# First batches loaded ahead of the weights, the start written out step by step, and the up weights' lower parts moved from GpSimd to VectorE

## The chip, the core and the metric

The kernel runs on one core of one Trainium2 chip. A core has a matrix engine (TensorE, "PE" in the rows, with its weight loads shown apart as "PEld"), a vector engine (VectorE, "DVE"), a scalar engine (ScalarE, "ACT"), GpSimd ("POOL") and a queue engine (SyncE, "SP") that here only issues DMAs. The engines run their own instruction streams in order and wait for one another through semaphores. The metric is the device time in microseconds, the median of three runs.

## The reference

```python
def _attn_ref(q, k, v):                       # (4, 8, 768, 64) each
    ...
    for t in range(S):
        state = gamma * state + einsum('bhd,bhe->bhde', k[:, :, t], v[:, :, t])
        y[:, :, t] = scale * einsum('bhd,bhde->bhe', q[:, :, t], state)

def _moe_ref(x, w_a, w_b, w_out):             # x 3072x512, d_ff 1536
    return (x @ w_a) * (x @ w_b) @ w_out

def _moe2_ref(x, w_gate, w_output_gate, w1, w2):   # 8 experts, 512 -> 1024 -> 512
    e_idx = argmax(x @ w_gate)
    ...
    out[mask] = gate_w * eom * (relu(x[mask] @ w1[e]) @ w2[e])
```

A decaying linear attention over 768 steps, a gated feed-forward layer, and a mixture of eight experts with one expert per token, chained on 3072 tokens, all in float32.

## The kernel before

**Blocks.** The tokens go through in seven blocks, block 0 to 6, most of 512 tokens. A block's feed-forward part loops over 12 slices `f` of the hidden width: `proj(j, f, 0, n)` and `proj(j, f, 1, n)` are two projections of 12 matmuls each, `gate` multiplies them, and `down` adds the slice into four accumulators with another 12 matmuls. Between them, in slots, stands the attention of the next block. So block 0 needs its own attention first, with nothing to overlap, and this stretch is called the start here.

**Three matmuls for one.** Every float32 operand is split into a high part (a cast by ACT) and a lower part (operand minus high part). `mm3` (L104 to L107) issues high by high, high by lower, lower by high. The first two need the high part of the weights, the third (L107) the lower part.

**The attention of a batch.** A batch is two heads pairs of 256 tokens. `load_batch(n)` brings two 512 KB tiles, `qk` and `vk`; `prep_q` and `prep_v` scale them (L139, L146) on DVE or POOL by the sets in L47; `scores` is 64 small matmuls in two tiles, masked by DVE (L189), with four running states added by DVE (L192) and a carry by POOL (L195); `outputs` is 64 small matmuls, two copies by ACT (L217) and two adds by DVE (L220). For block 0 the result `z` is then split into `xs` (L223 ACT, L224 DVE). Block 0 needs batches 0 to 3; the slots of block 0 do batches 4 to 7.

**Narrowing.** The weights of the feed-forward layer arrive as pairs of 32-bit words, 512 KB for each of 36 tiles. `narrow_all` (L473) makes floats of them: two reads by ACT (`narrow_a`, `narrow_r`), two joins by DVE (L487 and L489), then the high part by ACT (L457) and the lower part by POOL (L458). Twelve of the 36 are the down weights (`wos`), which are also written back to DRAM for later blocks; 24 are the up weights in `arena`. `narrow_all` is a generator, and `narrow(k)` advances it by k steps, from the third step of the start and three times per slice of block 0. A tile's slot in `wide` (4 deep) comes free with its second join, which is when `next_wide` issues the next load.

**Order.** All instructions are issued in the order in which the code is written (`tc.manual_schedule()`); the pools decide only the waits for buffers. Runs of small dummy matmuls (`keep_warm`, L783) stand between the steps of the start. SP issues the DMAs in order: batches 0 and 1, a weight tile, batch 2, three weight tiles, batches 3 and 4 (L786 to L799, L244).

Of the kernel before, what the change touches and what calls it, by code (L numbers as in the profile page):

```python
# [7 lines left out]
F32 = mybir.dt.float32  # L8
# [36 lines left out]
NARROW_FROM, CONST_AT = 2, 5  # L45

Q_POOL, V_POOL = {1, 2, 3}, {2, 3}  # L47
# [6 lines left out]
def attention_moe_moe2(ctx: ExitStack, tc: tile.TileContext, a: dict, out: bass.AP):  # L54
# [8 lines left out]
    e3 = early.enter_context(tc.tile_pool(name="e3", bufs=2))  # L63
    e5 = early.enter_context(tc.tile_pool(name="e5", bufs=3))
# [3 lines left out]
    def lp(n):  # L68
        if not late:
            for _ in narrowing:  # L70
                pass
# [64 lines left out]
    def prep_q(n):  # L136
        c, pp = batches[n]
        qd = p2.tile([128, 2, 256], F32, tag="qd", name="qd")
# [3 lines left out]
    def prep_v(n):  # L142
        c, pp = batches[n]
        vd = p2.tile([128, 2, 4, 64], F32, tag="vd", name="vd")
# [4 lines left out]
    spare = ["p0", "p1", "acc0", "acc1", "acc2"]  # L149

    def attn_bank(name):
        if not spare:
# [44 lines left out]
    def outputs(n, xr, toff):  # L197
# [20 lines left out]
        for i in range(2):  # L218
            zi = z[:, :, cols].rearrange("p k (j i n) -> p k j i n", j=2, i=2)[:, :, :, i]
            dve.tensor_tensor(zi, zi, y[i][:, 256:].rearrange("p (k j n) -> p k j n", k=2, j=2), op=ALU.add)  # L220
        if xr is None:
            hi, lo = (xs[:, w, 2 * pp : 2 * pp + 2, toff : toff + 256] for w in range(2))
            act.copy(hi, z)  # L223
            dve.tensor_tensor(lo, z, f32(hi), op=ALU.subtract)  # L224
# [7 lines left out]
    def attention_steps(j):  # L232
        own = [(ci, 2 * c + pp) for ci, c in enumerate(BLOCKS[j]) for pp in range(2)]

        def put(ci, n):
            if j == 0:
                xraw[j] = None
            elif j not in xraw:
# [3 lines left out]
        def s_a(n):  # L242
            scores(n)
            m = {0: 3, 1: 4, 2: None}.get(n, n + 2)  # L244
            if m and m < len(batches):
                load_batch(m)
# [7 lines left out]
        if j == 0:  # L254

            for i, (ci, n) in enumerate(own):
                steps.append(lambda n=n: s_a(n))
                if i:
                    steps.append(lambda p=own[i - 1], nxt=n + 1: s_b(*p, nxt if nxt <= len(own) else None))
            steps.append(lambda: s_b(*own[-1], None))  # L260
        else:
            for i, (ci, n) in enumerate(own):

                nxt = n + 1 if n + 1 < len(batches) and not (j == 1 and i + 1 == len(own)) else None
                steps.append(lambda n=n: s_a(n))
# [739 lines left out]
```

## Time and profile before

| | us |
|---|---|
| median of three runs | 1033.81 (1032.15 to 1034.11) |
| profiled execution | 1037.62 |
| its span, first to last instruction | 1035.7 |
| PE busy in the span | 1003.5 |
| start of the first projection matmul of block 0 | 37.14 |
| start of the second projection of slice 0 | 43.28 |
| start of the first projection of slice 1 | 46.15 |
| start of the first projection of block 1 | 155.74 |

The span is one profiled execution, 3.8 us slower than the median; some 1.9 us of the execution's time lie outside the span. A row of the timeline gives start, duration, engine, line, operation, tiles, and in brackets how long the engine had been idle before it and which instruction ended that. A group row gives busy time, mean duration in nanoseconds, and the idle time before. Matmuls are pipelined: one of 512 columns is shown as 0.39 us long, but the next starts some 0.23 us after it.

### The profile page before, as it was taken

What the parts mean: (1) busy time and instruction counts of PE and PEld (TensorE: products, weight loads), DVE (VectorE), ACT (ScalarE), POOL (GpSimd) and SP (SyncE); (2) the same over time, 40 slices, a digit from 0 to 9 for tenths busy, and PEclk for the clock granted to TensorE, in tenths of its full rate; (3) what the DMA queues carried; (4) which work ended last, traced back from release to release, by engine and by line L of the source; (5) the groups of instructions that cost most, each with busy time, mean ns of one, the idle gap of its engine ahead of it and who ended that gap; (6) DMA issues with size and microseconds to landing.
All of it is one profiled execution on the core that took longest, in us unless ns stands there. A gap on an engine that the chain in (4) does not pass through costs nothing. (4 is left out here: it accounts for less than half of the span.)

```text
span 1035.7 us, 20318 instructions
## 1 busy us (share of the span) xinstructions
PE 1003.5 (97%) x7701; PEld 840.1 (81%) x7702; DVE 606.6 (59%) x1383; ACT 382.3 (37%) x775; POOL 276.8 (27%) x241
## 2 busy tenths in 40 slices
PE   6799999999999999999999999999999999999997
PEld 4687778887888788888888888999899888789886
DVE  5799886755577547664775584453355444345441
ACT  3466662222322242223222323453354434344431
POOL 1455541113211421123113334341321120221211
PEclk7799999999999999999999999999999999999999
DMA  8676745322432342234221432360564552545620
GB/s 328 204 235 209 227 131 169 135 81 55 154 112 81 94 163 93 82 98 138 83 92 52 127 99 72 119 188 31 155 209 144 176 173 84 182 129 162 187 87 28
DMA packets 51640, 138.99 MB, mean 134 GB/s; under 512 B 10909, under 2 KB 11165, under 8 KB 51488
## 3 DMA queue, kind: packets, MB, share of 16 engines
q1 hardware_dynamic: 43920, 117.16, 35.3%
q0 software_dynamic: 6864, 19.46, 6.0%
q8 instruction: 85, 1.39, 0.5%
q10 hardware_dynamic: 720, 0.57, 0.2%
q14 instruction: 51, 0.42, 0.1%
HBM read 121.37 MB, written 16.70 MB: 133 GB/s over the span
## 5 line engine op out<-in xcount | busy, mean ns | idle before, releaser
L105 PE MATMUL p<-xs,arena 128*128 128x512 f32 (+1 forms) x672 | 248.5, 370 | 8.1 <-DVE z L220 4.2
L107 PE MATMUL p<-xs,arena 128*128 128x512 f32 (+1 forms) x672 | 242.5, 361 | 0.6 <-POOL arena L458 0.6
L106 PE MATMUL p<-xs,arena 128*128 128x512 f32 (+1 forms) x672 | 242.5, 361 | 0.0
L515 POOL TENSOR_TENSOR wos<-wo,wos 128x512 fp32r<-128x512 f32 x72 | 99.5, 1383 | 282.7 <-ACT wos L514 280.1
L105 PEld LDWEIGHTS p<-xs,arena 128*128 128x128 f32 x672 | 127.2, 189 | 31.8 <-issue 9.6
L107 PEld LDWEIGHTS p<-xs,arena 128*128 128x128 f32 x672 | 127.3, 190 | 20.7 <-POOL arena L458 1.0
L106 PEld LDWEIGHTS p<-xs,arena 128*128 128x128 f32 x672 | 127.5, 190 | 18.7
L542 ACT CAST gs<-g_sb 128x512 fp32r<-128x512 f32 (+1 forms) x84 | 47.0, 559 | 211.8 <-DVE g_sb L540 209.5
L340 DVE SCALAR_TENSOR_TENSOR junkd<-x,wcol 128x512 bf16<-128x512 f32 x144 | 122.0, 847 | 3.6
L105 PE MATMUL acc<-wos,gs 128*128 128x512 f32 x288 | 115.5, 401 | 0.0
L107 PE MATMUL acc<-wos,gs 128*128 128x512 f32 x288 | 113.3, 393 | 0.0
L106 PE MATMUL acc<-wos,gs 128*128 128x512 f32 x288 | 112.8, 392 | 0.0
L671 DVE TENSOR_TENSOR arena<-wraw,arena 128x512 fp32r<-128x512 f32 x112 | 76.2, 689 | 56.5 <-ACT arena L670 48.7
L637 DVE SCALAR_TENSOR_TENSOR hs<-ph,hs 128x384 fp32r<-128x384 f32 (+4 forms) x72 | 39.0, 542 | 113.6 <-ACT hs L636 87.7
L540 DVE TENSOR_TENSOR g_sb<-p,a_sb 128x512 f32<-128x512 f32 (+1 forms) x84 | 51.3, 611 | 79.4 <-PE p L107 70.2
L657 POOL DMA_INDIRECT out<-y,idx x27 | 27.5, 1018 | 234.9 <-ACT y L656 193.4
L105 PE MATMUL acc<-arena,hs 128*128 128x512 f32 (+1 forms) x216 | 86.1, 399 | 3.6 <-issue 1.9
L670 ACT CAST arena<-wraw 128x512 fp32r<-128x512 f32 x112 | 68.0, 616 | 57.7 <-PE acc L107 42.2
L107 PE MATMUL acc<-arena,hs 128*128 128x512 f32 (+1 forms) x216 | 85.8, 397 | 0.0
L106 PE MATMUL acc<-arena,hs 128*128 128x512 f32 (+1 forms) x216 | 85.3, 395 | 0.0
L543 DVE TENSOR_TENSOR gs<-g_sb,gs 128x512 fp32r<-128x512 f32 (+1 forms) x84 | 52.1, 620 | 52.5 <-ACT gs L542 51.2
L636 ACT ACTIVATE hs<-ph 128x384 fp32r<-128x384 f32 (+4 forms) x72 | 34.5, 479 | 127.0 <-PE ph L107 106.9
(147 smaller groups left out, 1687.0 us busy)
## 6 DMA issues: line engine op xcount, KB each, us to landing
wraw<-in_ex SPq DMA_DIRECT2D x64, 512.0 KB, 3.7
wo<-wo_d SPq DMA_DIRECT2D x72, 256.0 KB, 2.6
wide<-in_w_ab SPq DMA_DIRECT2D x24, 512.0 KB, 4.3
qk<-in_qk SPq DMA_DIRECT2D x23, 512.0 KB, 4.2
vk<-in_vk SPq DMA_DIRECT2D x23, 512.0 KB, 6.8
wcol<-in_wgt SPq DMA_DIRECT2D x20, 512.0 KB, 4.5
wide<-in_w_out SPq DMA_DIRECT2D x12, 512.0 KB
x_d<-x SPq DMA_DIRECT2D x24, 256.0 KB, 2.1
```

The costliest lines, as they stand in the source:

```text
L105: pe.matmul(outp, lhsT=wh, rhs=rh, start=start, stop=False)
L106: pe.matmul(outp, lhsT=wh, rhs=rl, start=False, stop=False)
L107: pe.matmul(outp, lhsT=wl, rhs=rh, start=False, stop=stop)
L340: dve.scalar_tensor_tensor(junk, x2t[i], 1.0, wc[:, e], op0=ALU.mult, op1=ALU.mult, accum_out=st["lg"][:, e0 + e : e0 + e + 1])
L515: pool.tensor_tensor(w[:, 1], t, f32(w[:, 0]), op=ALU.subtract)
L540: dve.tensor_tensor(g[:, :n], pb[:, :n], ta[:, :n], op=ALU.mult)
L542: act.copy(gs[:, 0, :n], g[:, :n])
L543: dve.tensor_tensor(gs[:, 1, :n], g[:, :n], f32(gs[:, 0, :n]), op=ALU.subtract)
L636: act.activation(h[:, 0, :n], p[:, :n], AF.Relu)
L637: dve.scalar_tensor_tensor(h[:, 1, :n], p[:, :n], 0.0, f32(h[:, 0, :n]), op0=ALU.max, op1=ALU.subtract)
L670: act.copy(arena[:, f, part, 0], t[:, part])
L671: dve.tensor_tensor(arena[:, f, part, 1], t[:, part], f32(arena[:, f, part, 0]), op=ALU.subtract)
```

## The change

The start is written out step by step in place of the loop over `attention_steps(0)`. Batches 0, 1 and 2 are loaded before the first weight tile, batch 3 before the second. Batches 2 and 3 have buffers of their own for their scaled operands (a `wos` buffer is borrowed), and both operands are scaled by POOL (`V_POOL` takes in 1). The first four batches use seven PSUM banks in turn, not five. `scores(n + 1)` stands in front of `outputs(n)`. `outputs` for block 0 hands back its three steps (join, high, lower), and the lower parts of batches 0 to 2 go to POOL, that of batch 3 to DVE. Narrowing has four functions of a tile's number: `n_read` (ACT), `n_join` (DVE, the first join now in place over the tile that ACT wrote), `n_high` (ACT), `n_low`. The lower part of an up weight is computed by DVE, that of a down weight by POOL. The reads run four tiles ahead, the joins three. The order of the 36 tiles has the down weight of a slice behind the up weights of the next one. The constants are loaded in slice 1 of block 0, not in the start.

```diff
-NARROW_FROM, CONST_AT = 2, 5
-
-Q_POOL, V_POOL = {1, 2, 3}, {2, 3}
+Q_POOL, V_POOL = {1, 2, 3}, {1, 2, 3}
...
-    e3 = early.enter_context(tc.tile_pool(name="e3", bufs=2))
-    e5 = early.enter_context(tc.tile_pool(name="e5", bufs=3))
+    e3 = early.enter_context(tc.tile_pool(name="e3", bufs=3))
+    e5 = early.enter_context(tc.tile_pool(name="e5", bufs=5))
...
+        if n in (2, 3):
+            both = p2.tile([128, 2, 512], F32, tag="wos", name="prep")
...
-    spare = ["p0", "p1", "acc0", "acc1", "acc2"]
+    spare = ["p0", "p1", "acc0", "acc1", "acc2", "gen", "gen"]
...
-    wide = [("ab", 0, 0), ("ab", 0, 1), ("wide", 0), ("ab", 1, 0), ("ab", 1, 1)]
+    wide = [("ab", 0, 0), ("ab", 0, 1)]
     for f in range(NF1):
-        wide += [("ab", f + 2, 0), ("ab", f + 2, 1)] if f + 2 < NF1 else [None, None]
-        wide += [("wide", f + 1)] if f + 1 < NF1 else []
-    wide = [k for k in wide if k]
+        wide += [("ab", f + 1, 0), ("ab", f + 1, 1)] if f + 1 < NF1 else []
+        wide += [("wide", f)]
...
+    def n_read(n):
+        if n < len(wide):
+            t = rawq[wide[n]]
+            e = e5.tile([128, 512], F32, tag="w_cv", name="w_cv")
+            act.activation(e, t[:, :, 1].bitcast(F32), AF.Copy, scale=REBIAS)
+            r = e3.tile([128, 512], I32, tag="r_cv", name="r_cv")
+            act.activation(r, t[:, :, 0].bitcast(U32), AF.Copy, scale=0.875 * 2.0**-29, bias=0.4999)
+            words[n] = e, r
+
+    def n_join(n):
+        if n < len(wide):
+            t = rawq.pop(wide[n])
+            w, r = words.pop(n)
+            wi = w.bitcast(I32)
+            dve.scalar_tensor_tensor(wi, wi, 3, r, op0=ALU.logical_shift_left, op1=ALU.bitwise_or)
+            dve.scalar_tensor_tensor(wi, t[:, :, 1], -0x80000000, wi, op0=ALU.bitwise_and, op1=ALU.bitwise_or)
+            whole[n] = w
+            next_wide()
+
+    def n_high(n):
...
+            act.copy(hi, w)
+            whole[n] = w, hi, lo, dve if key[0] == "ab" else pool
+
+    def n_low(n):
+        if n < len(wide):
+            w, hi, lo, eng = whole.pop(n)
+            eng.tensor_tensor(lo, w, f32(hi), op=ALU.subtract)
+
+    def narrow(n):
+
+
+        n_high(n + 2)
+        n_join(n + 3)
+        n_low(n + 2)
+        n_read(n + 4)
...
         load_batch(1)
+        load_batch(2)
         next_wide()
-        load_batch(2)
+        prep_all(0)
+        prep_all(1)
+        prep_all(2)
+        scores(0)
+        load_batch(3)
         next_wide()
         next_wide()
         next_wide()
...
+        scores(1)
+        load_batch(4)
+        prep_all(3)
+        keep_warm(WARM_STEP)
+        z0, h0, l0 = outputs(0, None, 0)
+        n_read(0)
+        z0()
+        h0()
+        l0(pool)
...
+        scores(3)
+        load_batch(5)
+        z2, h2, l2 = outputs(2, None, 256)
+        z2()
+        h2()
+        l2(pool)
+        n_join(0)
+        keep_warm(WARM_STEP)
+        z3, h3, l3 = outputs(3, None, 256)
+        keep_warm(2 * WARM_STEP)
+        n_high(0)
+        z3()
+        h3()
+        n_low(0)
+        l3(dve)
+        n_read(2)
+        n_join(1)
+        n_high(1)
+        n_low(1)
+        n_join(2)
+        n_read(3)
+        prep_all(4)
...
                 pa = proj(j, f, 0, n)
+                if j == 0:
+                    narrow(3 * f - (f > 0))
                 ta = act_a(pa, n)
-                if j == 0:
-                    narrow(4)
                 slot()
                 pb = proj(j, f, 1, n)
+                if j == 0:
+                    narrow(3 * f + 1 - (f > 0))
                 gate(j, f, ta, pb, n)
-                if j == 0:
-                    narrow(4)
...
                 if j == 0:
-                    narrow(4)
+                    if f:
+                        narrow(3 * f + 1)
+                    if f == 1:
+                        constants()
```

On SP at the very start, the DMA issues before are these (`stage` is batch 2's tile, `wide` a weight tile, the other `qk` and `vk` are batches 0, 1, 3 and 4):

```order
L130 DMA qk<-in_qk 128x1024
L131 DMA vk<-in_vk 128x1024
L130 DMA qk<-in_qk 128x1024
L131 DMA vk<-in_vk 128x1024
L433 DMA wide<-in_w_ab 128x1024
L130 DMA stage<-in_qk 128x1024
L131 DMA stage<-in_vk 128x1024
L433 DMA wide<-in_w_ab 128x1024
L433 DMA wide<-in_w_out 128x1024
L433 DMA wide<-in_w_ab 128x1024
```

and in the changed kernel these:

```order
L126 DMA qk<-in_qk 128x1024
L127 DMA vk<-in_vk 128x1024
L126 DMA qk<-in_qk 128x1024
L127 DMA vk<-in_vk 128x1024
L126 DMA stage<-in_qk 128x1024
L127 DMA stage<-in_vk 128x1024
L432 DMA wide<-in_w_ab 128x1024
L126 DMA qk<-in_qk 128x1024
L127 DMA vk<-in_vk 128x1024
L432 DMA wide<-in_w_ab 128x1024 x3
```

Both tiles of batch 2 now stand directly behind batch 1, and batch 3 behind a single weight tile; three weight tiles have moved behind batch 3.

On POOL, from its first scaling to the scaling of batch 4, before (`gc` is the carry of the state; `w_cv` a joined weight tile):

```order
L195 TENSOR_TENSOR state<-state,gc 128x128 x2
L139 TENSOR_TENSOR qd<-stage,dec 128x512
L195 TENSOR_TENSOR state<-state,gc 128x128
L139 TENSOR_TENSOR qd<-qk,dec 128x512
L458 TENSOR_TENSOR arena<-w_cv,arena 128x512
L195 TENSOR_TENSOR state<-state,gc 128x128
L458 TENSOR_TENSOR arena<-w_cv,arena 128x512
L139 TENSOR_TENSOR qd<-qk,dec 128x512
L146 TENSOR_TENSOR vd<-vk,vtab 128x512
L458 TENSOR_TENSOR wos<-w_cv,wos 128x512
```

and in the changed kernel (`prep` is the buffer for batches 2 and 3, `z` an attention output of block 0):

```order
L140 TENSOR_TENSOR prep<-stage,dec 128x512
L149 TENSOR_TENSOR prep<-stage,vtab 128x512
L201 TENSOR_TENSOR state<-state,gc 128x128 x2
L140 TENSOR_TENSOR prep<-qk,dec 128x512
L149 TENSOR_TENSOR prep<-vk,vtab 128x512
L234 TENSOR_TENSOR xs<-z,xs 128x2x256
L201 TENSOR_TENSOR state<-state,gc 128x128
L234 TENSOR_TENSOR xs<-z,xs 128x2x256
L201 TENSOR_TENSOR state<-state,gc 128x128
L234 TENSOR_TENSOR xs<-z,xs 128x2x256
L140 TENSOR_TENSOR qd<-qk,dec 128x512
L149 TENSOR_TENSOR vd<-vk,vtab 128x512
```

The scaling of batches 2 and 3 now stands before any weight work, with their `vd` halves, and the two lower parts of up weights have given way to three lower parts of `xs`.

On DVE, from the mask of batch 3 to the end of the start, before:

```order
L189 TENSOR_TENSOR m<-sc,mask 128x256 x2
L192 TENSOR_TENSOR state<-state,sc 128x128 x4
L487 SCALAR_TENSOR_TENSOR w_cv<-e_cv,r_cv 128x512
L489 SCALAR_TENSOR_TENSOR w_cv<-wide,w_cv 128x512
L220 TENSOR_TENSOR z<-z,y 128x4x64 x2
L224 TENSOR_TENSOR xs<-z,xs 128x2x256
L487 SCALAR_TENSOR_TENSOR w_cv<-e_cv,r_cv 128x512
L489 SCALAR_TENSOR_TENSOR w_cv<-wide,w_cv 128x512
L220 TENSOR_TENSOR z<-z,y 128x4x64 x2
L224 TENSOR_TENSOR xs<-z,xs 128x2x256
L487 SCALAR_TENSOR_TENSOR w_cv<-e_cv,r_cv 128x512
```

and in the changed kernel:

```order
L195 TENSOR_TENSOR m<-sc,mask 128x256 x2
L198 TENSOR_TENSOR state<-state,sc 128x128 x4
L228 TENSOR_TENSOR z<-z,y 128x4x64 x2
L466 SCALAR_TENSOR_TENSOR w_cv<-w_cv,r_cv 128x512
L467 SCALAR_TENSOR_TENSOR w_cv<-wide,w_cv 128x512
L228 TENSOR_TENSOR z<-z,y 128x4x64 x2
L487 TENSOR_TENSOR arena<-w_cv,arena 128x512
L234 TENSOR_TENSOR xs<-z,xs 128x2x256
L466 SCALAR_TENSOR_TENSOR w_cv<-w_cv,r_cv 128x512
L467 SCALAR_TENSOR_TENSOR w_cv<-wide,w_cv 128x512
L487 TENSOR_TENSOR arena<-w_cv,arena 128x512
L466 SCALAR_TENSOR_TENSOR w_cv<-w_cv,r_cv 128x512
```

Between the states of batch 3 and its join (the last `z<-z,y`) stood two pairs of weight joins and the join and lower part of batch 2; now it is one pair and the join of batch 2. The lower part of the first up weight now stands behind that join, on DVE.

## Rows read from the trace of the kernel before

**Rows 1.** Windows by stage: busy of each engine (instructions), granted clock, DMA share, GB/s.

```profile
37.00:42.00 5.00, 4.86 (x12) 3.75 (x12) 3.29 (x5) 1.72 (x3) 1.30 (x1) 0.53 0.59 188
42.00:156.00 114.00, 109.06 (x920) 86.31 (x919) 97.13 (x121) 73.18 (x134) 58.08 (x41) 1.00 0.62 197
156.00:1035.00 879.00, 865.79 (x6213) 732.19 (x6211) 482.22 (x1207) 294.84 (x614) 206.56 (x183) 1.00 0.38 119
```

**Rows 2.** Timeline of TensorE: scores of batch 2, block 0's first projections, block 1's first.

```profile
18.53 0.70 PE L185 MATMUL sc<-vd,stage 64*64 64x64 f32 x16 [1.66 <-DVE vd L146]
37.14 0.77 PE L105 MATMUL p<-xs,arena 128*128 128x512 f32 x1 [4.21 <-DVE z L220]
...
42.19 0.46 PE L181 MATMUL sc<-qd,qk 64*64 64x64 f32 x16
43.28 0.50 PE L105 MATMUL p<-xs,arena 128*128 128x512 f32 x1
46.15 0.39 PE L105 MATMUL p<-xs,arena 128*128 128x512 f32 x1
...
155.74 0.39 PE L105 MATMUL p<-xs,arena 128*128 128x512 f32 x1
```

**Rows 3.** Who TensorE waited for from 42 us to 157 us: us, times, longest.

```profile
PE p L105 <- DVE g_sb L540: 3.2, 4, 1.1
```

**Rows 4.** The DMA rate while the first batches load, as windows give it.

```profile
4.00:22.00 18.00, 12.05 (x324) 9.29 (x326) 11.31 (x29) 5.05 (x10) 2.02 (x3) 0.79 1.03 405
```

**Rows 5.** Timeline of SP: issue of batch 2's first tile.

```profile
6.85 0.33 SPq L130 DMA_DIRECT2D stage<-in_qk  x1
```

**Rows 6.** The same tile's view: time from issue to landing.

```profile
DMA to landing us min/median/max: 7.6/7.6/7.6
```

**Rows 7.** Timeline of POOL: the scaling of that tile.

```profile
15.10 1.27 POOL L139 TENSOR_TENSOR qd<-stage,dec 128x512 f32<-128x512 f32 x1
```

**Rows 8.** Groups by line up to 156 us: busy, mean ns, idle before.

```profile
L146 POOL TENSOR_TENSOR vd<-vk,vtab 128x512 f32<-128x512 f32 x4 | 5.1, 1274 | 0.0
L139 POOL TENSOR_TENSOR qd<-qk,dec 128x512 f32<-128x512 f32 x5 | 7.8, 1553 | 0.0
L189 DVE TENSOR_TENSOR m<-sc,mask 128x256 f32<-128x256 f32 x16 | 6.0, 413 | 0.3 <-PE sc L185 0.3
L192 DVE TENSOR_TENSOR state<-state,sc 128x128 f32<-128x128 f32 x26 | 7.4, 285 | 0.8
L217 ACT COPY z<-y 128x256 f32<-128x256 f32 x8 | 2.6, 374 | 14.9 <-PE y L211 14.9
L220 DVE TENSOR_TENSOR z<-z,y 128x256 f32<-128x256 f32 x8 | 3.0, 417 | 1.9 <-ACT z L217 1.9
L487 DVE SCALAR_TENSOR_TENSOR w_cv<-e_cv,r_cv 128x512 int32<-128x512 int32 x36 | 47.8, 1329 | 7.5 <-POOL arena L458 5.9 <-DMA wo_d<-w_cv 1.4
L489 DVE SCALAR_TENSOR_TENSOR w_cv<-wide,w_cv 128x512 int32<-128x512 int32 x36 | 35.0, 973 | 0.7
L457 ACT CAST arena<-w_cv 128x512 fp32r<-128x512 f32 x24 | 14.8, 616 | 1.9 <-DVE w_cv L489 1.9
L441 ACT ACTIVATE e_cv<-wide 128x512 f32<-128x512 f32 x36 | 24.2, 672 | 8.6 <-DVE w_cv L487 7.0 <-DMA wide<-in_w_ab 1.7
L543 DVE TENSOR_TENSOR gs<-g_sb,gs 128x512 fp32r<-128x512 f32 x12 | 8.4, 703 | 8.2 <-ACT gs L542 8.2
L458 POOL TENSOR_TENSOR arena<-w_cv,arena 128x512 fp32r<-128x512 f32 x24 | 36.6, 1528 | 24.8 <-ACT arena L457 24.8
L458 POOL TENSOR_TENSOR wos<-w_cv,wos 128x512 fp32r<-128x512 f32 x12 | 16.1, 1340 | 29.9 <-ACT wos L457 29.9
```

**Rows 9.** Timeline, a lower part on POOL and a join on DVE beside it, a join alone.

```profile
99.90 1.34 POOL L458 TENSOR_TENSOR wos<-w_cv,wos 128x512 fp32r<-128x512 f32 x1 [1.94 <-ACT wos L457]
99.98 1.80 DVE L487 SCALAR_TENSOR_TENSOR w_cv<-e_cv,r_cv 128x512 int32<-128x512 int32 x1
...
103.42 0.68 DVE L487 SCALAR_TENSOR_TENSOR w_cv<-e_cv,r_cv 128x512 int32<-128x512 int32 x1
```

More of the change, by code (lines that the diff above doesn't have):

```diff
@@ L147, in prep_v @@
         prep[n, "v"] = vd
-    spare = ["p0", "p1", "acc0", "acc1", "acc2"]
+    spare = ["p0", "p1", "acc0", "acc1", "acc2", "gen", "gen"]
     def attn_bank(name):
+        if spare and spare[0] == "gen":
+            spare.append(spare.pop(0))
+            return psg.tile([128, 512], F32, tag="gen", name=name)
         if not spare:
@@ L217, in outputs, with join_z @@
             act.copy(z[:, r, cols], y[r][:, :256])
[L218 to L224, printed above, removed]
+        def join_z():
+            for i in range(2):
+                zi = z[:, :, cols].rearrange("p k (j i n) -> p k j i n", j=2, i=2)[:, :, :, i]
+                dve.tensor_tensor(zi, zi, y[i][:, 256:].rearrange("p (k j n) -> p k j n", k=2, j=2), op=ALU.add)
+        if xr is not None:
+            join_z()
+            return None
+        hi, lo = (xs[:, w, 2 * pp : 2 * pp + 2, toff : toff + 256] for w in range(2))
+        return join_z, lambda: act.copy(hi, z), lambda eng: eng.tensor_tensor(lo, z, f32(hi), op=ALU.subtract)
     xraw = {}
@@ L243, in s_a @@
             scores(n)
-            m = {0: 3, 1: 4, 2: None}.get(n, n + 2)
-            if m and m < len(batches):
-                load_batch(m)
+            if n + 2 < len(batches):
+                load_batch(n + 2)
         def s_b(ci, n, nxt):
@@ L253, in attention_steps @@
         steps = []
-        if j == 0:
[L256 to L265, printed above, removed]
-                steps.append(lambda ci=ci, n=n, nxt=nxt: s_b(ci, n, nxt))
+        for i, (ci, n) in enumerate(own):
+            nxt = n + 1 if n + 1 < len(batches) and not (j == 1 and i + 1 == len(own)) else None
+            steps.append(lambda n=n: s_a(n))
+            steps.append(lambda ci=ci, n=n, nxt=nxt: s_b(ci, n, nxt))
         return steps
@@ L500, in attention_moe_moe2 @@
-    narrowing = narrow_all()
-    def narrow(k):
-        for _ in range(k):
-            next(narrowing, None)
+    def n_read(n):
[6 more added lines that the diff above has]
+            words[n] = e, r
@@ L799, in attention_moe_moe2, with constants @@
         next_wide()
[L800 to L819 removed]
+        scores(1)
[8 more added lines that the diff above has]
+        keep_warm(WARM_STEP)
+        scores(2)
+        z1, h1, l1 = outputs(1, None, 0)
+        n_read(1)
+        z1()
+        h1()
+        l1(pool)
+        scores(3)
[5 more added lines that the diff above has]
+        n_join(0)
+        keep_warm(WARM_STEP)
+        z3, h3, l3 = outputs(3, None, 256)
[12 more added lines that the diff above has]
+        prep_all(4)
+        spare.clear()
+        tri_f = p2.tile([128, 2, 128], F32, tag="wo", name="tri_f")
+        def constants():
+            sync.dma_start(tri_f, a["tri"])
+            sync.dma_start(base8, a["base8"])
+            sync.dma_start(ident, a["ident"])
+            sync.dma_start(wg, a["wg"])
+            sync.dma_start(iota8, a["iota8"])
+            sync.dma_start(pay, a["pay"])
+            sync.dma_start(tab_d[:, :], a["tab0"])
         tok0 = 0
```

95 lines of the change are left out of this document (23 added, 72 removed).

## The prediction

> **What bounds the kernel now.** I read the windows by stage first. From block 1 on, TensorE is busy 865.8 of 879 us, at a granted clock of 1.00 [rows 1], and the change touches nothing there: what it wins or loses must lie before 156 us and is then handed down unchanged. So I looked at TensorE's timeline up to there. Block 0's first projection matmul starts at 37.14, held back 4.2 us by the join of `z` (L220), the second projection at 43.28, the first of slice 1 at 46.15, and block 1 begins at 155.74 [rows 2]. Two stretches are of interest: the start, in which TensorE waits, and block 0, in which it is busy 109.1 of 114 us [rows 1] with most of its waiting for `g_sb`, 3.2 us in four pieces [rows 3]. In a wait the last matmul shown still covers some 0.16 us (0.39 shown for a pitch of 0.23), so six or seven short stops make the 4.9 idle microseconds about 6. DVE is the neighbour that is late in block 0: 97.1 us busy [rows 1] and 8.2 more waiting for ACT between the two halves of `gate` [rows 8], 105 of 114.
>
> **The start: when batch 3 is ready.** Before, scores of batch 2 stop 1.66 us for `vd`, which stands on DVE behind other work [rows 2]. Now POOL scales batches 2 and 3 as they land, so landing counts. DMA moves 405 GB/s [rows 4], 1.3 us for a 512 KB tile. Batch 2's first tile was issued at 6.85 and took 7.6 us, so it landed at 14.5 [rows 5, 6]. In the new order its second tile has the same bytes ahead of it (batches 0 and 1, the decay tables, one more tile) and I put it at 14.5 as well; one weight tile and batch 3's two follow at 1.3 us each: 18.4. I take POOL's scaling of a `vk` tile at its mean, 1.27 us [rows 8], of a `qk` tile at 1.27 as when nothing is in the way [rows 7]. Batch 2 is then done at 15.8 (bounds 14.2 and 17.4, if the tiles come 1.3 us earlier or later), batch 3 at 19.7.
>
> **The start: from there to the projections.** A scores step takes 1.09 us at the high clock (42.19 to 43.28, [rows 2]), of which 0.8 is left when `vd` comes: 20.5. Two masks of 0.41 and four states of 0.29 on DVE [rows 8]: 22.5. The last states feed the last of `outputs`, some 0.9 us: 23.4. Two copies of 0.37 by ACT: 24.1. On DVE the join of batch 2 comes after the states and ends at 23.2; the first weight join follows, and the second meets the lower part of `xs` on POOL (it starts at 23.9, after ACT's high part, and lasts 1.3), so it ends at 25.8 and batch 3's join at 26.4. ACT's high part of the first weight, 0.62, gives the first projection matmul at 26.5. Its third matmul needs DVE's lower part (27.1, or 27.6 if POOL scales batch 4 first), its eighth the lower part of batch 3's `xs`: between 27.8 and 29.3, I take 28.5. The other five matmuls end at 29.7, scores of batch 4 at 30.8. The second projection needs the second weight: joins to 29.9, high part 30.5, lower part 31.2. It runs from about 31.2, where before it was 43.28. Then one new stop: `a_sb`, which frees the PSUM bank for slice 1, stands on ACT behind the high part of the third tile (its join ends at 32.4, so 33.0) and two reads of 0.67 [rows 8], and so ends at 34.9, a microsecond after the second projection. Slice 1 starts at 34.9 in place of 46.15: **11.2 us gained**. Two smaller edits lie in this sum: the constants' DMAs, now in slice 1, were never waited for, and the in-place join has the operands of the old one.
>
> [...]
>
> **Block 0 after slice 0.** Here the question is DVE. A join lasts 0.68 us alone and 1.80 beside a POOL lower part [rows 9]; the 72 joins lasted 82.8 us [rows 8], 33.8 more than 72 times 0.68. POOL ran 36 lower parts and some 10 scalings meanwhile: about 0.74 us of held DVE for each. 24 of these go: 17.8 us less. DVE gets 24 lower parts of 0.70 (as L543, the same operation [rows 8]): 16.8 more. That is a draw, within 1 us over the block. Gone is one 5.9 us wait of the joins for a buffer that POOL still read [rows 8]; new is that the pipeline of tiles is shorter when slice 1 begins: three joined, five before, at most two tiles of 2 x 0.68 + 0.70, or 4.1 us, to be made up. I take TensorE's stops at 5 us, 1 less than now, with bounds of none (6 gained) and 10 (4 lost). Where I cost DVE's lower part at nothing for TensorE, the down matmuls of the slice before hide it; without them it costs 0.7 us per projection.
>
> What decides is whether the two engines exclude each other. Rows first: the join that began 0.08 us after POOL's lower part ended 0.54 us after it, while the joins of `z`, with one operand in PSUM, keep their 0.42 us mean all through [rows 8, 9]. [...]
>
> **Sum.** 11.2 + 1 = 12.2 us off the profiled execution's 1037.6 (3.8 above the median): 1025.4; off the median, 1021.6.
>
> **Rivals.**
> [...]
> *The stops go too* (over 16): if POOL, with half its work, stops holding DVE, the 5.9 us wait and the `g_sb` waits vanish together: 12.2 at the start with no new stop, 5 of the 6 in the block, 17.2, so 1016.6.
> *DVE becomes the bound, slower*: both projections of the 11 later slices wait, in their third matmul, for a lower part that POOL has held 1.1 us (1.80 less 0.68, [rows 9]), behind `gate` in DVE's queue: 22 x 1.1 = 24 us, less the 6 of now, less 11.2: 7 slower, 1041. It turns from gain to loss at 0.8 us per projection. For it: DVE is at 105 of 114 already. Against: the sum above is a draw.
> *Nothing moves*: the time won at the start is waited out at the end of block 0, since the 36 tiles cannot be narrowed faster than DVE did it before. For: the same 105. Against: that needs 11 us more of DVE in the block, and the joins that the start did before and does not do now are two tiles' worth, 4.1 at most. 1033.8.
>
> **How the numbers follow.** Forecast (9 to 16 us gained) 0.62, start gives less 0.18, stops go too 0.10, nothing moves 0.04, slower 0.06. A measurement here tells 0.2%, 2 us, from no change. So faster 0.90, same 0.04, slower 0.06. The likeliest case spans 1018 to 1025; for 8 in 10 I add the better part of the next two: 1016.5 to 1028.5.
>
> **What would show it.** First projection matmul of block 0 near 26.5 and of slice 1 near 35; `vd` of batch 3 on POOL ending near 19.7, with no TensorE wait for DVE's `vd`; one stop for `a_sb`; joins at a mean of 0.9 instead of 1.15 us; block 1's first matmul near 143.5; every later stage as long as before. I am wrong if block 0 from slice 1 on lasts over 112 us, with third matmuls (L103 in the changed file) waiting for DVE, or if batch 3 lands after 20.

## The result, and the profile after

The changed kernel takes 1024.09 us (median of 6 runs, 1023.61 to 1026.70), the kernel before 1033.40 beside it (6 runs, 1032.15 to 1034.50): a ratio of 0.9915, 95% interval 0.9905 to 0.9926, or about 9 us. The forecast was 12.2 us off, 1021.6; faster, and in the range, but a quarter of the gain is missing. The change was run a second time later (label e8_after_again): 0.9900, interval 0.9886 to 0.9914.

Where the time went is read best from four moments of TensorE (us from the span's start):

| | before | forecast | after | after again |
|---|---|---|---|---|
| first projection matmul | 37.14 | 26.5 | 29.05 | 29.96 |
| first of slice 1 | 46.15 | 34.9 | 38.27 | 39.83 |
| first of block 1 | 155.74 | 143.5 | 145.92 | 147.46 |
| slice 1 to block 1 | 109.59 | 108.6 | 107.65 | 107.63 |
| block 1 to the end of the span | 879.96 | as before | 876.28 | 875.04 |

The last line is code that the change leaves alone. It differs from execution to execution and from chip to chip (883 in one experiment below), so of the 13.6 us between the two profiled executions 9.8 lie ahead of block 1, where the change is, and 3.7 behind it, in code that is the same. Below, the moment of block 1 says what an edit did, and the ratio whether it reached the end.

TensorE's timeline after, which answers to [rows 2]: start, duration, line, operands, count, and in brackets its idle time with the cause.

```profile
17.07 0.65 PE L217 MATMUL y<-m,vd 64*64 64x64 f32 x30
20.57 0.32 PE L217 MATMUL y<-m,vd 64*64 64x64 f32 x2 [2.85 <-issue]
...
24.48 0.48 PE L217 MATMUL y<-m,prep 64*64 64x64 f32 x4 [0.83 <-issue]
...
29.05 0.47 PE L101 MATMUL p<-xs,arena 128*128 128x512 f32 x1 [0.20 <-DVE z L228]
...
30.53 0.50 PE L103 MATMUL p<-xs,arena 128*128 128x512 f32 x1 [0.78 <-DVE arena L487]
...
38.27 0.50 PE L101 MATMUL p<-xs,arena 128*128 128x512 f32 x1 [0.83 <-ACT a_sb L526]
...
145.92 0.39 PE L101 MATMUL p<-xs,arena 128*128 128x512 f32 x1
```

The first two brackets are what no step of the forecast had: TensorE stands still in the middle of batch 1's outputs, two matmuls before their end, and again four before the end of batch 2's, and no semaphore explains it ("issue"). The batches were not late. POOL scaled the last half of batch 3 here, ending at 18.73 where the forecast had 19.7:

```profile
17.69 1.04 POOL L149 TENSOR_TENSOR prep<-vk,vtab 128x512 f32<-128x512 f32 x1
...
28.65 1.28 POOL L140 TENSOR_TENSOR qd<-qk,dec 128x512 f32<-128x512 f32 x1
29.89 1.49 POOL L149 TENSOR_TENSOR vd<-vk,vtab 128x512 f32<-128x512 f32 x1
```

The last two rows are batch 4's. VectorE's lower parts of the first weight and of batch 3's `xs` run beside them and last 1.32 and 1.53 us in place of 0.69; this is called the hold here:

```profile
29.16 1.32 DVE L487 TENSOR_TENSOR arena<-w_cv,arena 128x512 fp32r<-128x512 f32 x1
30.40 1.53 DVE L234 TENSOR_TENSOR xs<-z,xs 128x512 fp32r<-128x512 f32 x1
...
33.94 0.69 DVE L487 TENSOR_TENSOR arena<-w_cv,arena 128x512 fp32r<-128x512 f32 x1 [0.69 <-ACT arena L481]
```

Stretches of the changed kernel, with the columns of [rows 1] (busy time and count of each engine, granted clock, DMA share, GB/s):

```profile
20.00:28.50 8.50, 7.10 (x202) 5.96 (x203) 4.53 (x13) 4.17 (x10) 3.41 (x4) 0.60 0.64 230
22.00:28.00 6.00, 5.17 (x131) 4.15 (x125) 3.85 (x11) 2.60 (x6) 2.60 (x3) 0.50 0.57 196
28.50:38.00 9.50, 7.95 (x83) 5.26 (x81) 8.71 (x13) 5.93 (x11) 2.88 (x3) 1.00 0.43 130
38.00:145.00 107.00, 103.47 (x844) 81.96 (x845) 95.81 (x145) 72.47 (x133) 29.82 (x20) 1.00 0.68 227
145.00:1022.00 877.00, 865.84 (x6218) 733.55 (x6216) 485.01 (x1208) 297.26 (x615) 207.54 (x183) 1.00 0.38 119
```

From 20 to 28.5 the mean granted clock is 0.60, and from 22 to 28 it is 0.50: it fell about a microsecond after the end of the first stop (1.00 from 21 to 21.5, 0.72 from 21.5 to 22). In the projections, from 28.5 to 38, it is 1.00. In block 0 POOL's busy time is halved (29.8 us, 58.1 before [rows 1]) and VectorE's is about what it was (95.8, 97.1 before). Who TensorE waited for up to 150 us (total, times, longest), beside [rows 3], and the groups that answer to [rows 8]:

```profile
PE p L103 <- DVE arena L487: 3.9, 6, 0.9
PE y L217 <- issue: 3.7, 2, 2.8
PE sc L191 <- DVE vd L149: 2.7, 2, 1.6
...
PE p L101 <- ACT a_sb L526: 0.8, 1, 0.8
```

```profile
L467 DVE SCALAR_TENSOR_TENSOR w_cv<-wide,w_cv 128x512 int32<-128x512 int32 x36 | 36.2, 1005 | 1.2
L466 DVE SCALAR_TENSOR_TENSOR w_cv<-w_cv,r_cv 128x512 int32<-128x512 int32 x36 | 28.1, 782 | 0.0
...
L487 DVE TENSOR_TENSOR arena<-w_cv,arena 128x512 fp32r<-128x512 f32 x24 | 17.0, 710 | 0.7 <-ACT arena L481 0.7
```

The two waits for `vd` are those of batches 0 and 1; batches 2 and 3 have none any more. The `g_sb` stops are gone, and third matmuls that wait for a lower part have come in their place: 0.78 us in slice 0, 0.93 and 0.89 in slice 2, 0.89 at 102 us and two shorter ones. The joins fell from 82.8 us [rows 8] to 64.3, a mean of 0.89; with 17.0 of lower parts that is 81.3.

### The profile page after: what moved, and what is told of

It reads as the page before. It is cut to its first block, busy times and chain, and to the rows that moved or that the text cites. A ratio compares the mean times of both kernels' runs of the same rounds, so it can differ in the third digit from the quotient of the medians.

```text
span 1022.2 us, 20303 instructions
## 1 busy us (share of the span) xinstructions
PE 997.1 (98%) x7692; PEld 836.7 (82%) x7693; DVE 603.0 (59%) x1402; ACT 384.0 (38%) x775; POOL 250.7 (25%) x222
```

## The experiments

Twelve runs, each beside runs of the kernel before on the same chip. Slice 1 of the combined kernels is taken from single records, since their rows are merged.

| run | first projection | slice 1 | block 1 | slice 1 to block 1 | ratio to before, interval |
|---|---|---|---|---|---|
| e1_lowers_pool | 29.69 | 44.77 | 153.86 | 109.09 | 0.9981, 0.9965 to 0.9996 |
| e2_before_dve | 36.94 | 45.89 | 149.73 | 103.84 | 0.9941, 0.9919 to 0.9962 |
| e3_less_traffic | 29.85 | 39.72 | 147.38 | 107.66 | 0.9922, 0.9899 to 0.9944 |
| e4_prep4_early | 30.57 | 38.89 | 145.94 | 107.05 | 0.9906, 0.9883 to 0.9928 |
| e5_no_warm | 27.85 | 37.72 | 145.34 | 107.62 | 0.9896, 0.9882 to 0.9910 |
| e6_low_last | 29.38 | 40.72 | 146.06 | 105.34 | 0.9903, 0.9889 to 0.9917 |
| e7_pool_from_third | 29.38 | 38.59 | 149.08 | 110.49 | 0.9935, 0.9923 to 0.9946 |
| e8_after_again | 29.96 | 39.83 | 147.46 | 107.63 | 0.9900, 0.9886 to 0.9914 |
| e9_combo | 27.95 | 36.9 | 142.68 | 105.8 | 0.9898, 0.9878 to 0.9919 |
| e10_combo_shift | 30.38 | 39.2 | 144.96 | 105.8 | 0.9914, 0.9897 to 0.9932 |
| e11_old_loads | 29.23 | 39.09 | 146.74 | 107.65 | 0.9942, 0.9925 to 0.9959 |
| e12_combo_again | 28.49 | 37.8 | 143.25 | 105.4 | 0.9875, 0.9856 to 0.9895 |

### What the lower parts on VectorE are worth

```diff
 e1, changed kernel:  -whole[n] = w, hi, lo, dve if key[0] == "ab" else pool
                      +whole[n] = w, hi, lo, pool
 e7, changed kernel:  +whole[n] = w, hi, lo, dve if n < 2 else pool
 e2, kernel before:   -pool.tensor_tensor(lo, w, f32(hi), op=ALU.subtract)
                      +(dve if key[0] == "ab" else pool).tensor_tensor(lo, w, f32(hi), op=ALU.subtract)
```

> The changed kernel with the lower parts of the 24 up weights of block 0 put back on GpSimd (POOL); everything else as changed. Theory (a draw on VectorE, as in the forecast): VectorE loses 24 x 0.71 = 17.0 us of lower parts and gets back about 24 x 0.74 = 17.8 us of holds in its joins (mean of the two join lines from 0.89 back to about 1.1 us); the time stays within 2 us of the changed kernel's 1024.1. Rival A (moving the lower parts is what made block 0 shorter): GpSimd's chain of lower parts delays the projections' third matmuls and the joins wait for buffers: 3 to 8 us slower, with new TensorE waits for POOL. Rival B (the change does worse with them on VectorE): 2 us faster or more.

> The kernel before with one part of the change alone: the lower parts of the 24 up weights go to VectorE, in the old order and with the old start. Theory (draw): within 2 us of before's 1033.4, joins at a mean near 0.9 in place of 1.15 us, the joins' 5.9 us wait for a buffer gone, the TensorE waits in block 0 about 5 us as before. Rival A (the move alone carries part of the gain): 2 to 6 us faster, as the 5.9 us wait goes and TensorE's g_sb stops (4.9 us) with it. Rival B (VectorE becomes the bound in the old order): 3 us or more slower, third matmuls of the projections wait for VectorE.

> The changed kernel with the lower parts of the up weights on GpSimd from the third tile on; the two of slice 0, on which the start hangs, stay on VectorE. With all of them on GpSimd slice 1 began at 44.77 in place of 38.27, since batch 4's scaling stood behind two of them in GpSimd's queue, so that the time of the block could not be read off. Theory (in the new order the lower parts on VectorE are a draw: less hold, more work): slice 1 begins at 38 to 40, slice 1 to block 1 takes 107 to 110, and the time is 0 to 3 us longer than the changed kernel's. Rival A (they are worth in the new order what they are in the old one, where moving them alone made slice 1 to block 1 5.75 us shorter): 4 to 7 us longer. Rival B (GpSimd, otherwise idle, would have done better): 1 us or more shorter.

The draw fell. The move alone (e2) makes the kernel before 0.59% faster, 6 us, at the upper end of its rival A; taken out of the change (e1) it leaves 0.2%. Who TensorE waited for up to 165 us in e1, the largest row of the first projections:

```profile
PE sc L187 <- POOL qd L140: 3.4, 1, 3.4
```

Two weights' lower parts stood ahead of batch 4's scaling in GpSimd's queue, and behind that wait, through most of the second projection, a matmul came every 0.43 us (40.74 to 43.72) in place of 0.23. So slice 1 began 6.5 us late, and only 1.4 us of the loss is in the block. e7, which spares slice 0 that queue, starts slice 1 with the changed kernel. From there to block 1 it takes 2.8 us more by the trace (110.49 against 107.65). That stretch repeats well: it is 107.62 to 107.66 in the traces of the changed kernel, e3, e5, e8 and e11. In the medians e7 is 3.8 us slower (1027.47 against 1023.64 side by side), which by the two intervals is known to some 2 us only. So the move is worth about 3 us in the new order, at the upper end of the theory and short of rival A's 4. TensorE's waits in e7 from slice 1 to block 1, and in e2 from 44 to 149 us:

```profile
PE p L103 <- POOL arena L487: 3.9, 4, 1.8
...
PE acc L102 <- POOL wos L487: 0.8, 2, 0.5
```

```profile
PE p L105 <- DVE g_sb L540: 0.8, 1, 0.8
```

And VectorE's groups in e2:

```profile
L487 DVE SCALAR_TENSOR_TENSOR w_cv<-e_cv,r_cv 128x512 int32<-128x512 int32 x36 | 35.9, 998 | 0.3
L489 DVE SCALAR_TENSOR_TENSOR w_cv<-wide,w_cv 128x512 int32<-128x512 int32 x36 | 28.0, 777 | 0.7
L458 DVE TENSOR_TENSOR arena<-w_cv,arena 128x512 fp32r<-128x512 f32 x24 | 19.4, 809 | 1.0 <-ACT arena L457 1.0
```

Joins and lower parts together are 83.3 us, against 82.8 for the joins alone before [rows 8]: in VectorE's busy time the move is the draw that was forecast. What went is the joins' wait for a buffer that GpSimd still read (5.9 us [rows 8], now 0.3) and the holds beside its lower parts, and all but one of TensorE's stops went with them. That the move did this is shown; which of the two did more is not. In the kernel before, 4.35 of the 5.9 us lie at 45.37, ahead of no `g_sb` stop; the other stands ahead of one, and the join that it delays is held too. A third row shows a held join without such a wait, 2.5 us ahead of the `g_sb` stop that ends at 137.95 (VectorE, TensorE, VectorE):

```profile
124.53 1.77 DVE L487 SCALAR_TENSOR_TENSOR w_cv<-e_cv,r_cv 128x512 int32<-128x512 int32 x1 [1.53 <-POOL arena L458]
...
128.37 0.47 PE L105 MATMUL p<-xs,arena 128*128 128x512 f32 x1 [1.13 <-DVE g_sb L540]
...
135.42 1.78 DVE L487 SCALAR_TENSOR_TENSOR w_cv<-e_cv,r_cv 128x512 int32<-128x512 int32 x1
```

In e2, with the old depth and order of tiles, block 0 from slice 1 on takes 103.84 us with one stop; the changed kernel's 107.65 is 3.8 above that.

### Why block 0 is not as short as that

```diff
 e6, block 0 only:
-    mm3(p, arena[.., 0, kk], arena[.., 1, kk], xs[:, 0, k], xs[:, 1, k], ...)
+    pe.matmul(p, lhsT=arena[.., 0, kk], rhs=xs[:, 0, k], ...)
+    pe.matmul(p, lhsT=arena[.., 0, kk], rhs=xs[:, 1, k], ...)
+for k in range(KD):
+    pe.matmul(p, lhsT=arena[.., 1, kk], rhs=xs[:, 0, k], ...)
```

> The changed kernel with the matmuls of block 0's projections in another order: the four that use the lower part of the weight come after the eight that use its high part, so that the lower part is needed 1.4 us later. Theory (in the changed kernel block 0 from slice 1 on, 107.65 us, is 3.8 us longer than the 103.84 of the kernel before with VectorE's lower parts alone, because fewer tiles are ahead when slice 1 begins and VectorE's lower parts come late in slices 1 to 3): the L103 waits (0.78 in the start, 0.93, 0.89, 0.16 and shorter ones after, 3.9 in all) go to under 1 us, slice 1 to block 1 takes 104 to 106, and the time is 2 to 4 us shorter. Rival A (VectorE sets the pace whatever TensorE's order: the wait moves to the projections' first matmul or to g_sb): within 1 us. Rival B (the lower part's waits are no more than a filler for other late work): the start keeps its time too.

From slice 1 to block 1 it takes 105.34, 2.3 less, as the theory said, and TensorE's waits there are these:

```profile
PE p L522 <- ACT arena L481: 1.0, 2, 0.5
PE acc L102 <- POOL wos L487: 0.7, 2, 0.3
PE p L527 <- DVE arena L487: 0.3, 1, 0.3
```

So 2.3 of the 3.8 us are the third matmuls' waits. That the tiles are late because fewer of them are ahead when slice 1 begins is not shown: the waits are not in slice 1 but in slice 2, at 102 us and later, and the changed kernel differs from e2 in the order of the tiles and of the steps too. The time did not move (0.9903): slice 1 began 0.9 to 2.5 us later than in the changed kernel's two traces, after a wait of 1.05 in slice 0 for the lower part of `xs`, which the new order needs sooner, and with a mean granted clock of 0.60 from 32 to 36.

### What stops TensorE in the start

```diff
 e3:  -load_batch(3); next_wide() x3; scores(1); load_batch(4)
      +load_batch(3); next_wide();    scores(1)
      ... +load_batch(4) ahead of scores(3), next_wide() x2 behind load_batch(5)
 e5:  -keep_warm(WARM_STEP)   (three places, before the last group of six)
```

> The changed kernel with 1 MB of weight tiles (the third and fourth) loaded behind batch 5 in place of ahead of batch 4. In the changed kernel's trace TensorE stops for nothing that a semaphore explains at 17.50 (3.06 us between two instructions) and at 23.34 (1.14 us), exactly 256 instructions apart, and at 17.99 and 22.00 a 16 KB packet of the queue called instruction begins, while the data queue is full up to 22. Theory (the instruction packet stands behind the data): with DMA full only until about 19.5 the first stop shrinks by 0.5 to 2.5 us and the second goes to below 0.8; block 1 begins 1 to 3 us earlier, 1021 to 1023. Rival A (the stop has a length of its own: the packet's 1.1 us and its latency, whatever else is moved): both stops as they are, 1024.1 within 1. Rival B (the weight tiles, now later, become the wait): the third tile lands after 29.9, the reads of ScalarE wait, and the time is 1 to 3 us longer.

> The changed kernel without the three groups of three warming matmuls on the attention path of the start (18 TensorE instructions; the 24 at the very start and the six ahead of the first projection stay). In the traces so far TensorE stops at instructions 705 and 961 of its stream whatever else was moved, and each time goes on 1.47 us after the end of a 16 KB packet of the instruction queue. Theory (the stop belongs to a place in the instruction stream, and the packet takes 4 to 5 us from TensorE's crossing of the boundary before): both stops move by the instructions taken out: the first falls after 4 matmuls of batch 3's scores in place of 2 ahead of the end of batch 1's outputs, so that ScalarE's copies of batch 1 no longer wait for it, the second out of batch 2's outputs; with that and 1.2 us of warming matmuls less, the first projection starts 0.5 to 2 us earlier and the time falls by as much. Rival A (the stop waits for data or for a clock step, not for instructions): it stays in front of the last two matmuls of batch 1's outputs. Rival B (the warming matmuls keep the clock up): stops move as said, but the granted clock is 0.5 in the first projections and they cost 2 us more: the time is level or 1 to 2 us longer.

> The changed kernel as it is, on the chip of this call, as the measure for the others and to see whether the start repeats. Theory: stops of TensorE again at the same two places of the instruction stream, 3 to 4 us together by the profile, first projection within 1 us of 29.05, slice 1 within 1 us of 38.27, block 1 within 1.5 us of 145.92; 0.991 to 0.992 of before. Rival (the two stops were an accident of one execution): no stop or another place, and block 1 about 3 us earlier.

Less traffic did not help (0.9922). The timeline of e3, then its windows from 18 us on (columns as above):

```profile
21.93 0.36 PE L217 MATMUL y<-m,vd 64*64 64x64 f32 x1 [4.07 <-issue]
...
26.21 0.33 PE L217 MATMUL y<-m,prep 64*64 64x64 f32 x4 [0.62 <-issue]
```

```profile
18.00:19.00 1.00, 0.00 (x0) 0.00 (x0) 0.81 (x3) 0.28 (x1) 0.98 (x2) 1.00 1.02 406
19.00:20.00 1.00, 0.00 (x0) 0.00 (x0) 0.00 (x0) 0.00 (x0) 1.00 (x2) 1.00 0.54 201
20.00:21.00 1.00, 0.00 (x0) 0.00 (x0) 0.00 (x0) 0.00 (x0) 1.00 (x2) 1.00 0.08 33
```

The data queue runs dry at about 19.5, and TensorE stands on for 2.4 us more. The changed kernel again (e8) stopped at the same two places, 4.06 and 0.71 us, with a DMA share of 1.03 from 16 to 20. So the stops are no accident. But slice 1 and block 1 came 1.6 and 1.5 us later than in the first trace, just outside what was expected, and the first stop differs by 1.2 us between these two executions of one kernel, as much as e3's does from the shorter of them. e5 moved the place. Its timeline:

```profile
17.67 0.33 PE L187 MATMUL sc<-prep,qk 64*64 64x64 f32 x2 [1.18 <-POOL prep L140]
20.83 0.40 PE L187 MATMUL sc<-prep,qk 64*64 64x64 f32 x11 [2.83 <-issue]
```

With six matmuls less ahead of it, the stop has moved out of batch 1's outputs and stands behind the first two matmuls of batch 3's scores (four were expected), so ScalarE's copies of batch 1 are free of it. The first projection came 1.2 and 2.1 us sooner than in the two traces of the changed kernel, block 1 0.6 and 2.1, as expected; in the time (0.9896 against 0.9900 side by side) it does not show. In the changed kernel's trace the first stop comes after 705 of TensorE's records (weight loads, matmuls and a few others) and the second after 961: 256 apart, 126 of them matmuls. In e5 TensorE also stood 126 matmuls after its first stop, at 24.74. In the changed kernel a packet of the queue named instruction begins at 17.99 and another at 22.00, here in a window of 0.2 us around the first (packets, MB, share):

```profile
q1 hardware_dynamic: 26, 0.08, 103.6%
q8 instruction: 1, 0.02, 33.9%
```

It is 16,384 bytes and takes 1.08 us, the second 1.04, and TensorE goes on 1.50 us after the end of the first and 1.44 after the end of the second. That TensorE waits for these packets is the author's reading of this order; what a packet holds, the trace does not show. From record 450, 256 ahead of the one behind the first stop, to that one took 5.3 us in the changed kernel (15.31 to 20.57), from there to the next instruction behind the second stop 3.9 (20.57 to 24.48). In the other ten traces that show a second stop this latter way took 3.6 to 4.3 us. In e11 TensorE did not stop there: the last 32 matmuls of batch 2's outputs, among which the second stop stands in the changed kernel, ran through from 24.87 on, 4.0 us after the end of the first stop at 20.87. In the kernel before, a like packet ended at 19.62; with 1.47 us more, the mean of the two above, TensorE could have gone on at 21.09 by the author's estimate, 6.3 us after record 450 (14.82), but there it reached record 705 only at 22.23 and did not stop. The changed kernel gets there at 17.50, 2.2 us after record 450.

What sets the length of that way is open. In the changed kernel the packets began 2.7 us after record 450 and 1.4 after the end of the first stop. Data traffic does not sort the second way: it took 3.9 us in the changed kernel with the DMA engines full at its start (shares of 1.03 and 0.94 in the two microseconds from 20), and 4.3 in e3 with next to no data moving (shares of 0.00 and 0.06 from 22 to 24; 21.93 to 26.21). For the first stop e3 does not settle it, since data still moved in its first part (a share of 1.02 from 18 to 19).

### GpSimd's hold, and the order of the loads

```diff
 e4:  +prep_all(4) behind scores(3), -prep_all(4) behind n_read(3)
 e11: -load_batch(2); next_wide() ... load_batch(3); next_wide() x3
      +next_wide(); load_batch(2); next_wide() x3 ... load_batch(3)
```

> The changed kernel with GpSimd's scaling of batch 4 moved ahead of the lower part of batch 2, so that it runs near 24.7 to 27.2 in place of 28.65 to 31.4, where it held VectorE's lower parts (1.32 and 1.53 us in place of 0.70). Theory (the hold is what delays the first projections): the first lower part of a weight ends at 29.9, the L103 wait of 0.78 us goes, the second up tile is joined 1.4 us earlier, the a_sb stop of 0.83 us goes too: slice 1 starts 1 to 2 us earlier and the time is 1022 to 1023. Rival A (moved, not removed): the first weight's joins (26.15 to 27.56) are held instead, the first projection starts 0.5 to 1 us later, and the time stays at 1024.1 within 1. Rival B (the gain is waited out in block 0, where the narrowing of the 36 tiles sets the pace): slice 1 earlier by 1 to 2 us, block 1 not.

> The changed kernel with the loads of the start in the order of before: one weight tile ahead of batch 2, three ahead of batch 3; everything else as changed. Batch 2 lands 1.3 us later, batch 3 3.9 us later (qk at 20.3, vk at 21.6 in place of 16.4 and 17.7). Theory (in the changed kernel TensorE is stopped for instructions until 20.6 to 22.1, so that most of the earlier landing goes unused): batch 3's scores end at 23 to 24.5 in place of 21.9 to 23.4, and the time is 1 to 2.5 us longer than the changed kernel's. Rival A (landing is what the start hangs on, as the forecast's walk has it): 3.5 to 4.5 us longer. Rival B (the order of the loads is nothing, the writing-out did it all): within 0.7.

e4 took the hold from the lower parts (0.69 us each again), and first projection to slice 1 fell from 9.22 to 8.32. But the first projection came 0.6 to 1.5 us later. The second stop was 1.93 us in place of 0.83, and VectorE's joins of the first weight were now held instead, as rival A said, 1.18 and 1.64 us in place of 0.68 and 0.69:

```profile
27.01 1.18 DVE L466 SCALAR_TENSOR_TENSOR w_cv<-w_cv,r_cv 128x512 int32<-128x512 int32 x1
28.22 1.64 DVE L467 SCALAR_TENSOR_TENSOR w_cv<-wide,w_cv 128x512 int32<-128x512 int32 x1
```

TensorE waited 1.48 us there, and its first projection matmuls came one every 0.43 us (31.16 to 33.29) in place of 0.23. So block 1 begins as before, and what the hold is worth by itself, a microsecond or more, the run does not show in the time.

In e11 batch 3 was ready 3.9 us later, and the start hardly saw it. Its POOL, then its TensorE:

```profile
21.58 1.05 POOL L149 TENSOR_TENSOR prep<-vk,vtab 128x512 f32<-128x512 f32 x1
```

```profile
20.87 0.32 PE L217 MATMUL y<-m,vd 64*64 64x64 f32 x2 [2.71 <-issue]
21.68 0.71 PE L187 MATMUL sc<-prep,qk 64*64 64x64 f32 x16 [0.49 <-POOL prep L140]
22.68 0.70 PE L191 MATMUL sc<-prep,vk 64*64 64x64 f32 x16 [0.30 <-POOL prep L149]
29.23 0.49 PE L101 MATMUL p<-xs,arena 128*128 128x512 f32 x1 [1.35 <-ACT arena L481]
```

Block 1 begins at 146.74, between the changed kernel's two traces: by the trace the earlier landing is used up by the stop. The ratio says 0.9942, 3 to 4 us longer. But all three kernels run side by side there (e9 to e11) took 882 to 884 us from block 1 on, 6 to 9 more than the changed kernel, and e9, one of them, came out 0.0023 better when it ran again on another chip (e12). Less that, 0 to 2 us are left. The trace speaks for the theory; the total does not settle it, since the changed kernel itself did not run beside them. What in the start did win the 8 us, own buffers, GpSimd's scaling or the steps written out, was not taken apart.

### Three edits together

```diff
 e9, e12: e5 and e4, and in block 0's projections
+parts = [(0, 0), (1, 0), (0, 1)] if f == 0 else [(0, 0), (0, 1), (1, 0)]
+for i, (wp, xp) in enumerate(parts): for k in range(KD): matmul(arena[.., wp, ..], xs[:, xp, k])
 e10: e9, and +keep_warm(32, 64) behind scores(0)   (32 matmuls of 64 columns)
```

> Three edits on the changed kernel together: no warming matmuls on the attention path of the start, GpSimd's scaling of batch 4 ahead of the lower part of batch 2, and in block 0's projections all matmuls with two high parts first (then, in slice 0, those with the weight's lower part, in later slices those with the data's lower part). Theory (what is left of the start is TensorE's instruction packets and GpSimd's hold, and block 0 from slice 1 on is held by lower parts that come late): first projection at 27.5 to 29.5, first projection to slice 1 in 8 to 9 us in place of 9.2 to 9.9, slice 1 to block 1 in 104 to 105.5 in place of 107.65; together 3 to 5 us off the changed kernel, 0.986 to 0.988 of before. Rival A (each of the edits only hands the wait on, as each alone left the time level): 0.989 to 0.992, level with the changed kernel. Rival B (the clock: with less to do TensorE is granted 0.5 through the projections): slower than the changed kernel by 1 to 2 us.

> The kernel of the expectation before with 32 small matmuls (64 columns, results not used) after batch 0's scores, where TensorE waits a microsecond for data anyway: they move all later 256-instruction boundaries 64 instructions ahead in the program. Theory (the packet is sent for when TensorE crosses the boundary before, and takes 4 to 6.5 us from there): the first stop moves from batch 3's scores to inside batch 1's outputs and ends 0.5 to 1.5 us earlier, the second stop too, first projection 0.5 to 1.5 us earlier, time 0.5 to 1.5 us shorter. Rival A (the packet comes at a time of its own, set by the DMA traffic, whenever it is sent for): the stops end when they ended, time the same within 0.7. Rival B (the small matmuls themselves hold up batch 1's scores): 0.5 to 1 us longer.

> The kernel with the three edits once more. In its first run block 1 began at 142.68, 3.2 to 4.8 us ahead of the changed kernel's two traces (145.92, 147.46), but the last 3000 or so matmuls, which no edit touches, took 5 to 7 us longer in all three runs of that call than in the two traces of the changed kernel, and the ratio to before was 0.9898. Theory (the early stage is 3 to 5 us shorter, the rest was the state of that chip): block 1 at 142 to 144 again; where the stages after it take 875 to 877 us as in the changed kernel's traces, the time is 1019 to 1021.5 and 0.985 to 0.988 of before. Rival (the gain does not repeat: block 1 at 145 or later, or the later stages are again longer than the changed kernel's by as much): 1023 or more, 0.989 to 0.992.

e12 takes 1021.78 us, 0.9875 of before: its interval lies below that of the changed kernel's first run and overlaps that of the second. e9, the same kernel at a time when every kernel took longer, was level with it (0.9898). Block 1 began at 142.68 and 143.25, 2.7 to 4.8 us ahead of the changed kernel, as expected. By the moment of block 1 it is the fastest version here. In the time it is ahead of the changed kernel by some 2 us in the medians, which were not taken side by side, and by the intervals it cannot be told from e5 or e6. TensorE in e12:

```profile
20.98 0.40 PE L187 MATMUL sc<-prep,qk 64*64 64x64 f32 x11 [2.16 <-issue]
...
25.24 0.69 PE L211 MATMUL y<-prep,state 64*64 64x64 f32 x32 [2.14 <-issue]
```

Both stops are still there. What was won lies in a first projection that came 0.6 to 2.0 us sooner, as in e5, and in block 0, 2 us from the new order of matmuls. In slice 0 nothing sure was won: first projection to slice 1 took 8.95 and 9.31 us, in e12 with a granted clock of 0.50 from 28 to 32, through most of the first projection. Its rival B had named that clock, but the loss of time that it put on it did not come. e10 put the stop where it was meant to:

```profile
14.17 0.62 PE L217 MATMUL y<-m,vd 64*64 64x64 f32 x26 [1.14 <-issue]
...
20.55 0.63 PE L217 MATMUL y<-m,vd 64*64 64x64 f32 x27 [3.82 <-issue]
```

But 126 matmuls earlier there was now a stop too, which ended at 14.17, and the stop that was to end sooner ended at 20.55, where in e9 it had ended at 20.44. It cost 2.3 us at block 1 and did not test what it was for.

## Why the prediction was right, and where it was wrong

**Landing (right).** Batches 2 and 3 were scaled 1 us sooner than forecast (batch 3 by 18.73 for 19.7), and the wait for VectorE's `vd` was gone. The bounds of batch 2 are a slip: 15.8 with 1.3 us either way is 14.5 and 17.1, and nothing hangs on them.

**"States 22.5, outputs of batch 3 end 23.4, z copies 24.1" (wrong).** This step let TensorE go on whenever its data was there. TensorE came to record 705 4.7 us sooner than before (17.50 for 22.23), and then it stood still, 3.7 us in the two stops. The clock took some more: at the granted 0.50 behind the first stop batch 3's outputs took 2.0 us (25.65 to 27.64), where in e8, at a mean of 0.85 from 24 to 28 and 1.00 after, they took 1.2 (27.02 to 28.19). The outputs of batch 3 ended at 27.6, and the first projection came at 29.05 in place of 26.5. That the stops go by a count of instructions is shown by e5 and e10, which moved them; that the packet is what they wait for is read from the changed kernel's records, in which they end 1.50 and 1.44 us after one. No run took the packet away.

**The projections to slice 1 (right in kind).** The hold by POOL was partly in the sum (third matmul at 27.6 at the latest, 1.1 after the first; it took 1.48); the `a_sb` stop was put at 1.0 and was 0.83. From first projection to slice 1 it took 9.22 where 8.4 was forecast. Together the start gained 7.9 of 11.2.

**"That is a draw" (wrong in what it was taken for).** As a sum of VectorE's time it was right to 1 us. But TensorE's stops hung on what GpSimd did to VectorE's joins, and the move that was priced at nothing is worth 5.75 us of block 0 in the old order (e2) and about 3 in the new (e7). The rest of the change loses in the block: 3.8 us beside e2, 0.9 where the lower parts stay on GpSimd (e7 beside the kernel before). The forecast put up to 4.1 on the shallower pipeline of tiles; e6 shows 2.3 us of waits for lower parts, and that the depth causes them is not shown. None of these terms was in the forecast of one microsecond for the block; that it came near the 1.9 measured is luck.

**Rivals.** The start did give less, though the tiles came early (batch 3 scaled by 18.73 for 19.7), and the clock was full in the two projections (1.00 from 28.5 to 38) and low only ahead of them, behind the first stop (0.50 from 22 to 28). What the range allows for a smaller gain was the author's estimate: no run shows the two projections of the changed kernel at the low clock, and its start gained 7.9 us. Of "the stops go too" one half came: the joins' wait for a buffer and the `g_sb` stops did vanish, but waits for lower parts took their place, 3.1 us from slice 1 on. VectorE as the bound shows only in these, five third matmuls of 22 projections, 0.9 us at most. The joins' mean of 0.9 us came as said, and the later stages are as long as before but for what differs between executions.

## What to carry to other kernels

When waits are taken out of a stretch of many small matmuls, count the instructions too: here TensorE ran 256 of them in 2.2 us and then stood still for 2.85, where the kernel before, with its waits, came to the same count 4.7 us later and did not stop. A sum of busy times does not tell what a move between engines is worth: here VectorE's sum was level (83.3 against 82.8 us in e2), and the move alone took 5.75 us from block 0. Making or undoing one part alone tells it. Where several edits each leave the time level, run them together before calling them useless: here three of them brought block 1 2.7 to 4.8 us forward, and about 2 us of that reached the time.

## What the runs showed of the hardware

In the changed kernel's trace TensorE stood still twice in the start, for 2.85 and 0.83 us, behind 705 and 961 of its records, and went on 1.50 and 1.44 us after the end of a packet of 16,384 bytes on the queue named instruction. From the end of the first stop to the end of the second it took 3.6 to 4.3 us in the traces that show both (6.4 between the first two stops of e10), and from record 450 to the end of the first stop 5.3 us in the changed kernel. The profile names nearly all of these stops "issue" (one of e5 is put down to PE). Six matmuls taken out ahead of the first stop (e5), or 32 put in ahead of the stops of e9 (e10), moved them to another step of the program.
